# Fifteen short transfers ahead of the tenth K tile of a decode kernel

## The chip, the cores and the metric

The kernel runs on one core of one Trainium2 chip. The metric is the device time of one execution in microseconds; of three runs before the change the median is 377.65 (377.62 to 378.11). A profile is of one execution of its own; "span" is the time from its first to its last instruction.

## The reference

One decode step of a transformer block for 4 sequences, in bfloat16: attention over a window of the cache, then a gated MLP, each after a layer norm and each added to its input.

```python
W = min(4096, max(256, Sk // 4))                       # 4096 of 16384 cached positions
q = (layernorm(x) @ wq)                                # x: 4 x 576, 32 query heads of 128
k, v = k_cache[:, :, Sk - W:, :], v_cache[:, :, Sk - W:, :]   # 4 x 16 KV heads x 4096 x 128
p = softmax(q @ k.T * 128 ** -0.5)                     # two query heads share one KV head
h = x + (p @ v).reshape(4, 4096) @ wo
gate, up = layernorm(h) @ W_gate, layernorm(h) @ W_up  # 576 x 4608 each
h2 = h + (gate * (gate > 0) * up) @ W_down
```

The arithmetic is small; the data is not. K and V are 64 MB each, and with the weights the kernel reads about 160 MB from memory.

## The kernel before

The work has 16 groups of four KV heads (`NTILE`), four for each sequence. A group has one K tile and one V tile of 128 partitions by 16384 elements, 4 MB each. All tiles lie in one large SBUF tensor, `arena`, which has two parts: a head for the spread-out queries, and four slots of 4 MB (`NSLOT`, `TILE`) that are used in turn by `ring_slot`. Into the slots go first the weight wq, then K0 to K3, then K and V alternately (K4, V0, K5, V1 and so on: V trails K by four groups), then the last four V tiles. wo, W_gate, W_up and W_down are loaded after them into the space that has become free; W_down comes in five pieces.

Nearly all transfers are issued by one engine, SyncE (SP), in the order of the calls of `P.dma("sync", ...)`; x alone is loaded from ScalarE's queue. `place` keeps for each block of 64 columns who read it last, and makes the new transfer wait for that reader: K9, the tenth K tile, waits for the QK matmuls of K7, whose slot it takes. `Prog` records operations in a queue for each engine and writes them out by `emit`; a wait stands in front of the instruction and holds up everything behind it on that engine. Each transfer adds 16 to a semaphore when it is complete. SyncE's order around the change is K8, V4, K9, V5.

VectorE transposes each K tile in place (`turn_k`, L424), TensorE multiplies it with the queries (`pe_qk`, L448 and L34). After the four groups of a sequence follow the row maximum (L453), the exponential (L467), a rearrangement of the probabilities (`remap`, L475, L482, L487) and, group by group, the product with V (`pe_pv`, L509 and L34) and the picking of the wanted rows (`select_o`, L519 to L526). At the end stand the product with wo (L617), the norm, gate and up (L666), and the product with W_down (L690), whose pieces are waited for one by one. Then the output, 4 rows, is stored from SyncE (L710), which waits for its arrival.

Of the kernel before, what the change touches and what calls it, by code (L numbers as in the profile page):

```python
# [9 lines left out]
BF16 = mybir.dt.bfloat16  # L10
# [110 lines left out]
def bass_sequential_preLN__sliding_block_cached__glu_gated_reglu__decode_kernel(  # L121
# [12 lines left out]
    with ExitStack() as es:  # L134
        cnt = [0]

        def sb(name, shape, dt):
            return es.enter_context(nc.sbuf_tensor("sb_" + name, shape, dt))

        P = Prog()  # L140
# [5 lines left out]

        PPW = 6144
        AW = 2 * QWW + NSLOT * TILE
        arena = sb("arena", [128, AW], BF16)
        pp = sb("pp", [128, PPW], BF16)  # L150
        ident_b = sb("ident_b", [128, 128], BF16)
# [64 lines left out]
        def place(name, off, size, reader, make, key=None):  # L216
            deps = []
            for blk in range(off // 64, (off + size) // 64):
                r = owner.get(blk)
                if r is not None and r not in deps:  # L220
                    deps.append(r)
                owner[blk] = reader
            semk = key or "d_" + "_".join(str(v) for v in name)
            P.dma("sync", ("L",) + name, make, semk, deps)
            land[name] = off
# [3 lines left out]
        def ring_slot():  # L229
            s = ring[0] % NSLOT  # L230
            ring[0] += 1
            return s


        def add_kv(kind, g):
            b, qd = divmod(g, 4)
            s = ring_slot()
            off = slot0 + s * TILE
            cache = A_k_cache if kind == "K" else A_v_cache
            src = cache[b, 4 * qd:4 * qd + 4, SK - WIN:SK, :].rearrange("a (p t) d -> p a (t d)", p=32)  # L240
            place((kind, g), off, TILE, ("QK", g) if kind == "K" else ("PV", g),
                  lambda e: e.dma_start(out=arena[:, off:off + TILE], in_=src), key=f"slot{s}")  # L242


        def main_rows(W):
            return W[0:512, :].rearrange("(p r) n -> p (r n)", r=4)

        def last_rows(W):
# [5 lines left out]
        place(("wq", 0), wq_off, TILE, "QMM",  # L254
              lambda e: e.dma_start(out=arena[:, wq_off:wq_off + TILE], in_=main_rows(A_wq)), key=f"slot{s}")  # L255
        for g in range(NTILE):
            add_kv("K", g)
            if g >= 4:
                add_kv("V", g - 4)
# [3 lines left out]
        for g in range(NTILE - 4, NTILE):  # L263
# [5 lines left out]
        place(("gu", 0, 4), off, F, ("GU", 1, 4), lambda e, off=off: e.dma_start(  # L269
            out=bass.AP(tensor=arena, offset=off, ap=[[2 * AW, 64], [1, F]]), in_=B_W_gate[512:576, :]))  # L270
        P.dma("sync", ("L", "gu", 1, 4), lambda e, off=off: e.dma_start(
            out=bass.AP(tensor=arena, offset=AW + off, ap=[[2 * AW, 64], [1, F]]), in_=B_W_up[512:576, :]), "d_gu_1_4")
        gu_off[(0, 4)] = gu_off[(1, 4)] = off
# [8 lines left out]
        for r0, r1 in zip(WD_ROWS, WD_ROWS[1:]):  # L282
            place(("wd", r0), wd_off + r0 * D, (r1 - r0) * D, ("DOWN", 1),
                  lambda e, r0=r0, r1=r1: e.dma_start(
                      out=arena[:, wd_off + r0 * D:wd_off + r1 * D],
                      in_=B_W_down.rearrange("(p r) n -> p (r n)", p=128)[:, r0 * D:r1 * D]))
# [18 lines left out]
                                                in_=c_qm[:, :, :].rearrange("p q (h j) -> p q h j", j=4),  # L305
# [4 lines left out]
                                                in_=to_v[:, :, :].rearrange("p n (k a) -> p n k a", a=4),  # L310
# [14 lines left out]
        for sg in range(2):  # L325
            pool(f"c_toq{sg + 1}", lambda e, sg=sg: e.affine_select(
                out=toq[:, :, :, :], in_=toq[:, :, :, :],
# [84 lines left out]
        def put_q():  # L412
            for i in range(4):
                for q in range(2):
                    act("QW", lambda e, i=i, q=q: e.copy(  # L415
                        out=bass.AP(tensor=arena, offset=32 * i * AW + 2 * i + q, ap=[[AW, 32], [512, 16], [136, 4], [32, 4]]),
                        in_=bass.AP(tensor=q_keep, offset=q, ap=[[512, 32], [32, 16], [8, 4], [2, 4]])),
# [9 lines left out]
        def pe_qk(g):  # L427
            b, qd = divmod(g, 4)
            for cb in range(4):
                for w in range(2):  # L430
                    for a in range(4):
# [8 lines left out]
                        lhsT = arena[:, b * 2048 + cb * 512 + g % 4 * 128 + a * 32:][:, 0:32]  # L440
                        rhs = bass.AP(tensor=arena, offset=off, ap=[[AW, 128], [128, 64], [16, 4], [4, 2]])
                        out_ = bank[w][32 * a:32 * a + 32, :]
# [98 lines left out]
        def finish_o():  # L541
            for q in range(4):
                for qd in range(4):
# [17 lines left out]
                                              in_=bass.AP(tensor=e8, offset=0, ap=[[8, 128], [0, 4], [1, 8]])), ["c_e8", "c_selc0"])  # L561
# [47 lines left out]
        for a in range(8):  # L609
            for n in range(2):  # L610
                for j in range(4):
# [4 lines left out]
                    else:  # L616
# [6 lines left out]
                                             in_=bass.AP(tensor=psb, offset=512 + 224, ap=[[4096, 128], [1, 64], [0, 2]])), ["part1"])  # L623
# [54 lines left out]
        for i in range(2):  # L678
            dve(("HHT", i), lambda e, i=i: e.transpose(
                out=hhT[:, 576 * i:576 * i + 576].rearrange("p (r q) -> p r q", q=32),  # L680
                in_=bass.AP(tensor=pp, offset=3712 + 18 * i, ap=[[PPW, 128], [1, 18], [36, 32]])), [("HH", m) for m in range(3)])
# [26 lines left out]
        dve("OUT0", lambda e: e.tensor_copy(out=out_sb[:, 0:272], in_=bank[0][0:32, 0:272]), [("DOWN", 0)])  # L708
        act("OUT1", lambda e: e.copy(out=out_sb[:, 272:576], in_=bank[1][32:64, 0:304]), [("DOWN", 1)])  # L709
        P.dma("sync", "O", lambda e: e.dma_start(out=out.rearrange("b s d -> (b s) d"), in_=out_sb[0:B, :]), "d_out", ["OUT1", "OUT0"])  # L710
        P.op("sync", None, None, ["O"])
        P.emit(nc, es)


# [26 lines left out]
```

## Time and profile before

| | |
|---|---|
| median of 3 runs | 377.65 us |
| the profiled execution | 378.22 us |
| its span | 377.0 us |
| read from memory | 159.58 MB, 423 GB/s over the span |
| DMA packets | 6378, of them 728 under 512 bytes |
| granted TensorE clock, mean | 0.796 |
| VectorE busy | 228.8 us (61%) |
| TensorE busy | 213.8 us (57%) |

A transfer is cut into packets, which 16 DMA engines work off side by side, each in the order of its queue. A slice in the row of the DMA shares is a fortieth of the span; the digit 9 stands for 90% and more. K tiles land in the median 26.3 us after their issue and V tiles after 28.5, since each stands behind earlier ones in the queue. SyncE's rows in the timeline are its issues.

### The profile page before, as it was taken

Reading aid. Unit: us, or ns where it says so; the run is one execution under the profiler, and the core shown is the slowest. Engines: PE = TensorE matmul, PEld = TensorE weight load, DVE = VectorE, ACT = ScalarE, POOL = GpSimd, SP = SyncE. Lnnn points to the kernel's source line nnn. Section 1 sums busy time; section 2 is a strip of 40 time slices with the busy share of each in tenths; the row PEclk is TensorE's granted clock in tenths of the full one; section 3 lists DMA queues with packets and bytes.
Section 4 is the critical chain, followed back from the end, with each engine's and each line's share of the span. In section 5 each row is a group of like instructions: output and inputs, shape, how many; then the busy total and the mean of one; then the engine's idle time right before and its main releaser. Section 6 shows DMA issues by size and latency. Waiting matters only on the chain.

```text
span 377.0 us, 2556 instructions
## 1 busy us (share of the span) xinstructions
PE 213.8 (57%) x1462; PEld 39.9 (11%) x694; DVE 228.8 (61%) x164; ACT 53.7 (14%) x84; POOL 10.5 (3%) x29
## 2 busy tenths in 40 slices
PE   0404443239919091749282844664655787886658
PEld 0000000001001010001010100110000101002316
DVE  4088878779292969584847778665749433333240
ACT  3093000211000114010101140101010411112010
POOL 8200000000000000000000000000000000000000
PEclk9966666659969788696877786989695968998686
DMA  8999999999999999999999999999999999999996
GB/s 334 445 445 428 405 445 442 396 442 445 398 435 445 442 433 403 442 445 435 407 436 445 435 414 431 441 438 431 417 442 438 426 417 442 418 433 437 427 414 256
DMA packets 6378, 159.74 MB, mean 424 GB/s; under 512 B 728, under 2 KB 864, under 8 KB 1248
## 3 DMA queue, kind: packets, MB, share of 16 engines
q1 hardware_dynamic: 6360, 159.59, 98.7%
q8 instruction: 8, 0.13, 0.1%
q14 instruction: 2, 0.02, 0.0%
q10 hardware_dynamic: 8, 0.00, 0.0%
HBM read 159.58 MB, written 0.00 MB: 423 GB/s over the span
## 4 chain that ended last, share of the span: by engine, by line
DMA 60%; PE 20%; DVE 18%; SPq 1%; issue 0%; ACT 0%
DMA sb_arena<-in_A_k_cache_dram 53%; DVE sb_arena L424 16%; PE psb L34 11%; DMA sb_arena<-in_B_W_down_dram 7%; PE psb L448 4%; PE psb L509 3%; PE psb L690 2%; DVE sb_o_tmp L522 1%; DVE sb_pp L487 1%; SPq L242 0%; PE psb L475 0%; SPq L255 0%; ACT sb_out_sb L709 0%; SPq L251 0%; DVE sb_f L534 0%
## 5 line engine op out<-in xcount | busy, mean ns | idle before, releaser
L424 DVE STREAM_TRANSPOSE sb_arena<-sb_arena 128x8192 f32<-128x8192 f32 (+1 forms) x19 | 139.9, 7366 | 67.3 <-DMA sb_arena<-in_A_k_cache_dram 67.3
L448 PE MATMUL psb<-sb_arena 128*32 128x512 bf16 x256 | 42.8, 633 | 119.6 <-DVE sb_arena L424 119.5
L34 PE MATMUL psb<-sb_arena,sb_pp 128*128 128x512 bf16 (+1 forms) x386 | 108.7, 392 | 0.0
L509 PE MATMUL psb<-sb_arena,sb_pp 128*128 128x512 bf16 x128 | 50.8, 397 | 8.9 <-DVE sb_o_tmp L522 8.9
L519 ACT COPY sb_o_tmp<-psb 32x512 f32<-32x512 f32 x32 | 18.5, 577 | 182.0 <-PE psb L34 181.7
L34 PE MATMUL psb<-sb_arena 128*32 128x512 bf16 x256 | 43.6, 642 | 0.0
L522 DVE TENSOR_TENSOR sb_o_tmp<-psb,sb_fm 32x512 f32<-32x512 f32 x32 | 21.7, 678 | 18.6 <-PE psb L34 18.1
L448 PEld LDWEIGHTS psb<-sb_arena 128*32 128x32 bf16 x256 | 9.5, 119 | 161.9 <-DVE sb_arena L424 132.7
L509 PEld LDWEIGHTS psb<-sb_arena,sb_pp 128*128 128x128 bf16 x128 | 12.8, 100 | 116.6 <-issue 116.6
L526 DVE TENSOR_REDUCE sb_o_sel<-sb_o_tmp 128x128 f32<-128x512 f32 x16 | 17.7, 1106 | 0.5
L467 ACT ACTIVATE sb_pp<-psb,sb_hx 128x1024 bf16<-128x1024 f32 x4 | 4.5, 1113 | 79.4 <-DVE sb_hx L464 79.4
L487 DVE TENSOR_TENSOR sb_pp<-psb,sb_m 128x1024 bf16<-128x1024 f32 x8 | 9.3, 1206 | 4.9 <-PE psb L475 4.9
L482 ACT ACTIVATE sb_pp<-psb,sb_m 128x512 bf16<-128x512 f32 x16 | 9.7, 690 | 14.9 <-PE psb L475 14.9
L525 DVE TENSOR_TENSOR sb_o_tmp<-sb_o_tmp,sb_fm 64x512 f32<-64x512 f32 x16 | 11.0, 689 | 0.5
L415 ACT COPY sb_arena<-sb_q_keep 32x256 bf16<-32x256 bf16 x8 | 9.7, 1451 | 0.1
L690 PE MATMUL psb<-sb_arena,sb_pp 128*32 128x272 bf16 (+1 forms) x70 | 7.6, 396 | 3.7 <-DMA sb_arena<-in_B_W_down_dram 3.7
L401 DVE CAST sb_pp<-psb 128x512 bf16<-128x512 f32 x1 | 2.4, 2427 | 10.5 <-PE psb L381 10.5
L470 DVE STREAM_TRANSPOSE sb_pp<-sb_pp 128x1024 bf16<-128x1024 bf16 x4 | 5.0, 1245 | 5.1 <-ACT sb_pp L467 5.1
L475 PE MATMUL psb<-sb_pp,sb_to_v 128*32 128x256 bf16 x64 | 4.3, 400 | 6.3 <-DVE sb_pp L470 6.3
L690 PEld LDWEIGHTS psb<-sb_arena,sb_pp 128*32 128x32 bf16 x70 | 6.0, 131 | 5.1 <-DMA sb_arena<-in_B_W_down_dram 3.9
L34 PE MATMUL psb<-sb_arena,sb_hnT 128*32 128x384 bf16 x80 | 6.5, 407 | 0.0
L381 PE MATMUL psb<-sb_arena,sb_xnT 128*32 128x512 bf16 x16 | 2.6, 628 | 6.3 <-DMA sb_arena<-in_A_wq_dram 6.3
(120 smaller groups left out, 81.5 us busy)
## 6 DMA issues: line engine op xcount, KB each, us to landing
sb_arena<-in_A_k_cache_dram SPq DMA_DIRECT2D x16, 4096.0 KB, 26.3
sb_arena<-in_A_v_cache_dram SPq DMA_DIRECT2D x16, 4096.0 KB, 28.5
sb_arena<-in_A_wo_dram SPq DMA_DIRECT2D x1, 4608.0 KB, 24.8
sb_arena<-in_B_W_gate_dram SPq DMA_DIRECT2D x1, 4608.0 KB, 27.7
sb_arena<-in_A_wq_dram SPq DMA_DIRECT2D x1, 4096.0 KB, 12.7
sb_arena<-in_B_W_up_dram SPq DMA_DIRECT2D x1, 3456.0 KB, 27.3
sb_arena<-in_B_W_down_dram SPq DMA_DIRECT2D x1, 2160.0 KB, 26.5
sb_arena<-in_B_W_down_dram SPq DMA_DIRECT2D x1, 1440.0 KB, 29.6
```

Of the source, the lines that this page charges most:

```text
L34: return e.add_instruction(mybir.InstMatmult(name=e.bass.get_next_instruction_name(), engine=mybir.EngineType.PE, ins=[e.lower_ap(rhs), e. ...
L415: act("QW", lambda e, i=i, q=q: e.copy(out=bass.AP(tensor=arena, offset=32 * i * AW + 2 * i + q, ap=[[AW, 32], [512, 16], [136, 4], [32, 4]]),
L424: dve(("TRA", g), lambda e: e.transpose(out=dst, in_=src), [("L", "K", g)] if lo == 0 else [])
L448: fn = lambda e, out_=out_, lhsT=lhsT, rhs=rhs, start=start, stop=stop: e.matmul(out_, lhsT=lhsT, rhs=rhs, start=start, stop=stop, skip_gr ...
L482: act(("EV", b, 0), lambda e, a=a: e.activation(out=bass.AP(tensor=pp, offset=2 * a, ap=[[PPW, 128], [8, 2], [32, 128], [1, 2]]), in_=bank ...
L487: dve(("EV", b, 1), lambda e, n=n: e.tensor_tensor(out=bass.AP(tensor=pp, offset=16 + 8 * n, ap=[[PPW, 128], [32, 128], [2, 4], [1, 2]]), ...
L509: fn = lambda e, lhsT=lhsT, rhs=rhs, k=k, j=j: e.matmul(bank[2 + j], lhsT=lhsT, rhs=rhs, start=(k == 0), stop=(k == 7), skip_group_check=True)
L519: act(("OSC", g), lambda e, j=j: e.copy(out=o_tmp[32 * j:32 * j + 32, 0:512], in_=bank[2 + j][32 * j:32 * j + 32, :]), [("PV", g), ("OSEL" ...
L522: dve(("OSD", g), lambda e, j=j: e.tensor_tensor(out=ot(32 * j, 32), in0=bank[2 + j][32 * j:32 * j + 32, :].rearrange("p (t d) -> p t d", ...
L525: dve(("OS", g), lambda e: e.tensor_tensor(out=ot(64, 64), in0=ot(64, 64), in1=fmb(64, 64), op=ALU.mult), [("OSC", g)])
L526: dve(("OSEL", g), lambda e: e.tensor_reduce(out=o_sel[:, qd, b, :], in_=o_tmp[:, 0:512].rearrange("p (t d) -> p d t", d=DH), axis=AX.X, o ...
L690: return lambda e: e.matmul(out_, lhsT=lhsT, rhs=w[:, lo:hi], start=start, stop=stop, skip_group_check=True)
```

## The change

A scratch tile `mark` of 128 partitions by 1024 elements is allocated ahead of `arena`. After V4's issue and before K9's, SyncE issues fifteen transfers into it. The k-th, k from 1 to 15, copies k rows of wq, 40 + k elements (82 to 110 bytes) of each, to every fourth partition from the first on, at column 64 k. Together they have 120 rows. They wait for nothing and share one semaphore. Nobody reads `mark`; SyncE alone waits for the marks, after the output.

```diff
+        mark = sb("mark", [128, 1024], BF16)
         arena = sb("arena", [128, AW], BF16)
...
         for g in range(NTILE):
+            if g == 9:
+                for k in range(1, 16):
+                    P.dma("sync", ("L", "mark", k), lambda e, k=k: e.dma_start(
+                        out=bass.AP(tensor=mark, offset=64 * k, ap=[[4 * 1024, k], [1, 40 + k]]), in_=A_wq[0:k, 0:40 + k]), "d_mark")
             add_kv("K", g)
             if g >= 4:
                 add_kv("V", g - 4)
...
-        P.op("sync", None, None, ["O"])
+        P.op("sync", None, None, ["O", ("L", "mark", 15)])
```

## The prediction

> **What bounds the kernel now.** I read the page first: busy shares and the row of DMA shares, then the queues, then the chain that ended last.
>
> ```profile
> PE 213.8 (57%) x1462; PEld 39.9 (11%) x694; DVE 228.8 (61%) x164; ACT 53.7 (14%) x84; POOL 10.5 (3%) x29
> ...
> DMA  8999999999999999999999999999999999999996
> ...
> q1 hardware_dynamic: 6360, 159.59, 98.7%
> ...
> DMA 60%; PE 20%; DVE 18%; SPq 1%; issue 0%; ACT 0%
> ```
>
> No compute engine is busy for more than 61%, but the 16 DMA engines are busy in every slice, and the packets of SyncE's queue alone fill 98.7% of 16 engines' span. What a DMA engine has to do more is time; what an issuing or computing engine has to do more is not, so long as that queue stays full.
>
> Next, when SyncE issues, around the edit and at the end:
>
> ```profile
> 115.80 0.54 SPq L242 DMA_DIRECT2D sb_arena<-in_A_k_cache_dram  x1
> 122.80 0.54 SPq L242 DMA_DIRECT2D sb_arena<-in_A_v_cache_dram  x1
> 135.22 0.54 SPq L242 DMA_DIRECT2D sb_arena<-in_A_k_cache_dram  x1
> 142.22 0.54 SPq L242 DMA_DIRECT2D sb_arena<-in_A_v_cache_dram  x1
> ...
> 375.64 0.33 SPq L710 DMA_DIRECT2D out_dram<-sb_out_sb  x1
> ```
>
> The columns are start, duration, instruction. These are K8, V4, K9 and V5. Between V4's issue (ends 123.34) and K9's, SyncE stands 11.88 us waiting for the QK matmuls of K7 to free a slot.
>
> Third, the end of the kernel in the timeline:
>
> ```profile
> 367.49 7.24 PEld L690 LDWEIGHTS psb<-sb_arena,sb_pp 128*32 128x32 bf16 x70 [3.93 <-DMA sb_arena<-in_B_W_down_dram]
> ```
>
> The last product starts when the first piece of W_down lands. A DMA engine that is late to the end moves the end one for one.
>
> Last, the trace's packet records, one by one. A tile of 4 MB is 8 packets of 32768 bytes on each engine and then one of 4 bytes, the semaphore's. Sorting those 4-byte records by time and taking 16 per transfer gives each engine's lateness. K0's are 0.34 us apart from first to last. K9's lie from 159.32 to 161.00, apart by 1.68: ten engines within 0.14, then 0.19, 0.33, 1.01, 1.33, 1.63, 1.68. At the first piece of W_down the spread is 1.79, and seven engines lie between 1.66 and 1.79. The lag comes from the ten instruction-block packets after the start (eight of 16384 bytes, about 1 us each, at 46.3, 96.5, 140.0 us and on; two of 8192): a block makes one engine late, and a late engine never catches up. So the end belongs to the latest engine, and extra work on an early engine is free up to its lead.
>
> **The change part by part.** It moves and removes nothing; it adds four things.
>
> Fifteen issues on SyncE, after V4 and ahead of K9. They have no wait, so they run in the 11.88 us gap. Short transfers' nearest row is the output's 0.33 us for 4 rows, the dearest usual row is the K tile's 0.54: 15 x 0.33 = 5.0 to 15 x 0.54 = 8.1 us. Both fit. Behind them on SyncE stands K9, then V5 and the rest. Should the gap not do, there is a second cover: K9's packets start only when V4's are through, 149.64 to 151.28, so K9 may be issued some 14 us late before a ring runs dry. I take 0. Neither a gain nor a loss follows before that.
>
> 120 short packets (82 to 110 bytes each) and 120 semaphore packets on the DMA engines. How they spread is the first unknown. The only short transfer of the kernel with its own queue is the load of x, 4 rows of 1152 bytes:
>
> ```profile
> q10 hardware_dynamic: 8, 0.00, 7.4%
> ```
>
> That is four rows and four semaphores, and their records overlap (data at 2491, 2510, 2514 and 2567 ns): four rows, four engines. So the mark with k rows should use k engines. The Trainium skill, "DMA: Bandwidth & Descriptors", section on why a DMA increments its semaphore by 16, says so too, and adds that they are the lowest-numbered k; the four overlapping packets agree on the number, no run here shows which. By it the first engine carries 15 marks, the next 14, the sixteenth none. If they rotated, each engine would carry 7.5 on average.
>
> The price of one mark on an engine. In the last piece of W_down, packets of 1152 bytes start 47 ns apart, those of 4096 bytes of wq 155 ns apart, a semaphore takes 6 ns. The line through the two gives 4.7 ns plus 0.0367 ns a byte, so 8 ns for 96 bytes; with the semaphore 14 ns. That is the lower end: 15 x 14 = 0.21 us on the busiest engine. At the full 1152-byte pitch it is 15 x 53 = 0.80 us. The upper end comes from ordering: the semaphore reaches its waiter 0.36 us after its packet (wq's first: packet at 13.18, event at 13.54). If each mark had to be complete before the next began, one costs 0.36 + 0.05 = 0.41, and 15 cost 6.2 us. I take 14 ns: the nearest rows are short packets in a saturated stream, and between pieces of W_down the next data packet starts 6 ns after a semaphore, with no gap.
>
> What of it counts. A mark's delay shows at the end only as far as its engine is then among the latest. With 0.21 us falling to 0 over the engines and seven engines within 0.13 us of the last, the end moves 0 to 0.21; I take 0.15.
>
> One more wait on SyncE after the output has landed. The marks were done 220 us before, so it costs an instruction: adjacent issues stand 0.05 us apart (0.80 + 0.40 to 1.25). I take 0.05.
>
> The scratch tile moves every later tile by 2048 bytes per partition; their alignment below 2048 stays. No row shows an effect of position on a transfer (K and V packets take 1.21 us in all four slots). 0.
>
> Sum: +0.20 us. The profiled execution took 378.22 us (span 377.0 and 1.22 around it), 0.57 above the median; 378.4 there, **377.85** against the median of 377.65. A measurement of this kernel tells about 0.2% (0.75 us) from no change.
>
> **The rivals.**
>
> A, slower: marks don't pipeline. Each engine finishes one mark's write before its semaphore, and that before the next mark. For it: no two semaphores in this trace follow each other closer on one engine than the last W_down piece (8 x 47 + 6 ns = 0.38 us), so the stream of marks is something the trace never shows. Against it: no gap after any semaphore that it does show. The place is the ring between V4 and K9. With 0.1 us a mark the busiest engine is 1.5 us later, with 0.2 3.0, with 0.41 6.2, less the lead that it has over the last engine (0 to 1.7, half of it taken, 0.9). That gives 378.3, 379.8 and 383.0. It decides from about 0.11 us a mark: (0.75 + 0.9) / 15. The Trainium skill, "DMA: Bandwidth & Descriptors", section "Queues, rings and completion order", states that a semaphore write lands only after every earlier write of its engine, which is what such a stall would come from; the trace agrees that it lands late, 0.36 us, but shows following data unhindered. The Trainium skill's "DMA: Bandwidth & Descriptors", section "Anatomy of one DMA", puts a fixed 2.0 us on each DMA (of another issue path); 15 of them one after the other would by that be an estimated 30 us, and the last two pieces of W_down, 0.38 us apart on an engine, disagree.
>
> B, faster: the latest engine is relieved. Mean lag at W_down's first piece is about 0.9 of 1.79 us. If 240 added packets shift which engine fetches which instruction block, or when, so that the late ones are spared, up to 0.9 us is to be had: 376.8. For it: the ten blocks now fall on different engines and the latest are bunched. Against it: TensorE's program, which needs the blocks, is unchanged. It decides only if nearly all of the bunch goes.
>
> C, slower: SyncE is held. If a mark takes over 0.79 us to issue (11.88 / 15), K9 is issued late, and over 1.87 us each ((151.28 - 123.34) / 15) the rings run dry behind V4: 15 x 2.5 us would leave them empty for some 10 us, 388. Every single issue in the timeline lies between 0.33 and 0.68 us, so this has little.
>
> D, it doesn't do what it says: all rows of a mark on one engine. 120 x 8 + 15 x 6 ns = 1.05 us there, 378.4 with half the lead absorbed; the x load's four engines speak against it.
>
> **How the numbers follow.** Forecast, within 0.2%: 0.52 (D's 0.02 lies inside). A 0.36, C 0.02: slower 0.38. B 0.10: faster. The range is 377.0 to 381.0: below it B's greater part (0.08), above it A from 0.28 us a mark, and C (0.11 together).
>
> **What would show it.** On SyncE 15 new issues between 123.3 and about 131, K9 still at 135.2. In the packet records 120 packets of 82 to 110 bytes near 150 us. Spread of K9's semaphores 1.7 to 1.9 us (forecast); 3 and more, and lasting to the end, means A; DMA share below 9 near 150 us means C. A K9 tile that lands by 161.2 and a product that starts at 367.5 to 367.9 confirm the sum. What would make it wrong: a price of a mark that no row here has, or another drawing of instruction blocks.

## The result and the profile after

The changed kernel takes 379.82 us (median of 4 runs, 379.54 to 380.1), the kernel before 377.63 beside it: 1.0055 of it, 95% interval 1.0039 to 1.0071, or 2.2 us slower. It lies inside the stated range, but 2.0 us above the forecast of 377.85, where the range had been widened for rival A. The profiled execution took 379.72 us, with a span of 378.4.

The page of the changed kernel, the lines that answer to those of before (busy times, DMA shares, the queue, the chain that ended last):

```profile
PE 208.3 (55%) x1447; PEld 39.4 (10%) x694; DVE 228.3 (60%) x164; ACT 53.7 (14%) x84; POOL 10.5 (3%) x29
...
DMA  8999999999999999999999999999999999999995
...
q1 hardware_dynamic: 6600, 159.60, 98.4%
...
DMA 57%; PE 21%; DVE 20%; issue 1%; ACT 0%; SPq 0%
```

The queue has 240 packets more (120 rows, 120 semaphores), and no slice in the middle is below 9: at this grain nothing is to be seen. SyncE's issues in the timeline:

```profile
122.30 0.53 SPq L243 DMA_DIRECT2D sb_arena<-in_A_v_cache_dram  x1
122.87 11.27 SPq L260 DMA_DIRECT2D sb_mark<-in_A_wq_dram  x15
134.54 0.60 SPq L243 DMA_DIRECT2D sb_arena<-in_A_k_cache_dram  x1
```

The fifteen issues fill 11.27 us, nearly all of the gap of 11.7 us, and K9 is still issued on time. K9's transpose on VectorE, before and then after:

```profile
161.48 8.71 DVE L424 STREAM_TRANSPOSE sb_arena<-sb_arena 128x8192 f32<-128x8192 f32 x1 [5.08 <-DMA sb_arena<-in_A_k_cache_dram]
```

```profile
163.14 8.71 DVE L429 STREAM_TRANSPOSE sb_arena<-sb_arena 128x8192 f32<-128x8192 f32 x1 [7.34 <-DMA sb_arena<-in_A_k_cache_dram]
```

The wait in the bracket is 2.26 us longer (the whole execution ran 0.6 us ahead of before's until then). The product with W_down, the last consumer, before and then after:

```profile
367.49 4.74 PE L690 MATMUL psb<-sb_arena,sb_pp 128*32 128x272 bf16 x38 [3.72 <-DMA sb_arena<-in_B_W_down_dram]
```

```profile
369.02 5.08 PE L695 MATMUL psb<-sb_arena,sb_pp 128*32 128x272 bf16 x50 [3.71 <-DMA sb_arena<-in_B_W_down_dram]
```

It starts at 369.02 in place of 367.49, although the execution had been 0.6 us ahead until K9. So the loss comes at the marks and stays to the end.

The packet records say where. In the kernel before, K9's last semaphore comes 9.72 us after V4's last; with the change 12.01 (150.68 to 162.70): 2.29 us lost. Since mark k has rows of 80 + 2k bytes, the records tell the engines apart: k rows lie on k engines, and the engine that first appears with mark 1 has 15 of them. Each row and its semaphore pass in 14 to 15 ns where the engine was early. But the first K9 packets behind them take up to 2.46 us in place of 1.21. The table shows when each engine's first mark starts, and by how much the time from there to K9's semaphore is longer than 8 undisturbed packets of 1.21 us:

```
marks on the engine      15    14    13    12    11    10     9     8     7     6     5     4     3     2     1
first mark at, us      0.53  0.56  0.54  1.58  0.09  1.86  1.83  0.00  0.18  2.07  0.23  0.22  0.18  0.25  0.33
lost from there, us    1.74  1.91  2.19  2.20  1.53  1.96  2.20  1.11  0.50  1.18  0.51  0.49  0.44  0.41  0.29
```

The first row is counted from the first mark of the earliest engine, at 148.98 us. The loss grows with the marks. The sixteenth engine has no mark and lost 0.26 us all the same, here and when the change was run again, so a small part of the loss is not an engine's own; where that part comes from was not tried. Of the four engines that were late already, by 1.49 to 1.71 us at V4's semaphores, three have 9 to 12 marks; they start on them up to 0.4 us after their V4 and then lose about 2 us each. They set K9's landing and, since no engine catches up, the end.

### The profile page after: what moved, and what is told of

The parts are those of the page before. It is cut to its first block, busy times and chain, and to the rows that moved or that the text cites. A ratio compares the mean times of both kernels' runs of the same rounds, so it can differ in the third digit from the quotient of the medians.

```text
span 378.4 us, 2556 instructions
## 1 busy us (share of the span) xinstructions
PE 208.3 (55%) x1447; PEld 39.4 (10%) x694; DVE 228.3 (60%) x164; ACT 53.7 (14%) x84; POOL 10.5 (3%) x29
## 4 chain that ended last, share of the span: by engine, by line
DMA 57%; PE 21%; DVE 20%; issue 1%; ACT 0%; SPq 0%
DMA sb_arena<-in_A_k_cache_dram 48%; DVE sb_arena L429 16%; PE psb L34 13%; DMA sb_arena<-in_B_W_down_dram 9%; PE psb L453 4%; PE psb L514 3%; DVE sb_o_tmp L527 1%; DVE sb_pp L492 1%; PE psb L480 1%; PE psb L695 0%; DVE sb_pp L475 0%; DVE sb_hx L458 0%; ACT sb_pp L472 0%; SPq L289 0%; SPq L256 0%
## 5 line engine op out<-in xcount | busy, mean ns | idle before, releaser
L34 PE MATMUL psb<-sb_arena,sb_pp 128*128 128x512 bf16 x384 | 106.3, 385 | 2.9 <-issue 2.8
L514 PE MATMUL psb<-sb_arena,sb_pp 128*128 128x512 bf16 x115 | 44.0, 383 | 9.0 <-DVE sb_o_tmp L527 9.0
L695 PE MATMUL psb<-sb_arena,sb_pp 128*32 128x272 bf16 (+1 forms) x70 | 6.7, 352 | 4.5 <-DMA sb_arena<-in_B_W_down_dram 4.5
L680 DVE TENSOR_TENSOR sb_pp<-psb,sb_pp 128x384 bf16<-128x384 f32 x3 | 1.5, 550 | 9.0 <-PE psb L671 9.0
L671 PE MATMUL psb<-sb_arena,sb_hnT 128*32 128x384 bf16 x40 | 4.2, 405 | 4.0 <-DMA sb_arena<-in_B_W_up_dram 2.0
L34 PE MATMUL psb<-sb_arena,sb_hnT 128*32 128x384 bf16 x80 | 6.2, 392 | 0.0
```

Of the source, the lines that this page charges most:

```text
L34: return e.add_instruction(mybir.InstMatmult(name=e.bass.get_next_instruction_name(), engine=mybir.EngineType.PE, ins=[e.lower_ap(rhs), e. ...
L514: fn = lambda e, lhsT=lhsT, rhs=rhs, k=k, j=j: e.matmul(bank[2 + j], lhsT=lhsT, rhs=rhs, start=(k == 0), stop=(k == 7), skip_group_check=True)
```

## The experiments

Three theories were put to the test. S: each small transfer's completion (its semaphore, on the engine) takes its time, one after another. P: an engine looks ahead a limited number of packets, and short ones use them up. L: rows under 512 bytes are slow in themselves. Beside these: the moved tiles, the shared semaphore, contention among all engines. "Lost by the mean engine" is the mean of K9's 16 semaphores less that of K8's, less two undisturbed tiles (19.41 us); in the kernel before it is 0.01 us, with the change 1.27. Each ratio is to the kernel before on the same chip, with the 95% interval.

**The tile alone.**

```diff
-            if g == 9:
-                for k in range(1, 16):
-                    P.dma("sync", ("L", "mark", k), lambda e, k=k: e.dma_start(
...
-        P.op("sync", None, None, ["O", ("L", "mark", 15)])
+        P.op("sync", None, None, ["O"])
```

> The scratch tile is allocated, no transfer is issued; the output is the reference's. If the loss comes from the transfers, the time is that of before, 377.6 +- 0.4 us. If it comes from the 2048 bytes by which every later tile is moved, it is 379.8 as with the change.

1.0001 (0.9992 to 1.001). Moving the tiles by 2048 bytes costs nothing.

**One transfer of 256 short rows.**

```diff
-                for k in range(1, 16):
-                    P.dma("sync", ("L", "mark", k), lambda e, k=k: e.dma_start(
...
+                P.dma("sync", ("L", "mark", 15), lambda e: e.dma_start(
+                    out=bass.AP(tensor=mark, offset=0, ap=[[1024, 128], [64, 2], [1, 48]]),
+                    in_=A_wq[0:256, 0:48].rearrange("(p r) n -> p r n", r=2)), "d_mark")
```

> One transfer of 256 rows of 96 bytes in place of the fifteen: 16 short packets and 1 semaphore on each engine. In the changed kernel's packet records an engine with 1 to 5 marks lost 0.3 to 0.5 us, one with 9 to 15 lost 1.2 to 2.2 us. Theory S (the completion of each small transfer costs, so the loss goes with the semaphores): one completion, 0.3 us lost on each engine, 377.9. Theory P (an engine looks ahead a limited number of packets, and short ones use them up, whatever they are): 17 packets, like 8 or 9 marks, 1.1 to 2.2 us lost, 378.7 to 379.8. Theory L (rows under 512 bytes are slow in themselves): 16 of them, at least as much as 15 marks, 1.7 to 2.2 us, 379.4 to 379.8.

0.9999 (0.999 to 1.0009). The mean engine lost 0.20 us, of which 16 rows at 8 ns and a semaphore are 0.13. 16 short packets on each engine with one semaphore do not stall it: P and L, as put, fall.

**Eight transfers of 16 rows.**

```diff
-                for k in range(1, 16):
+                for k in range(8, 16):
                     P.dma("sync", ("L", "mark", k), lambda e, k=k: e.dma_start(
-                        out=bass.AP(tensor=mark, offset=64 * k, ap=[[4 * 1024, k], [1, 40 + k]]), in_=A_wq[0:k, 0:40 + k]), "d_mark")
+                        out=bass.AP(tensor=mark, offset=(k - 8) * 1024, ap=[[8 * 1024, 16], [1, 48]]),
+                        in_=A_wq[0:128, 0:48].rearrange("(r j) n -> j r n", j=8)[k - 8]), "d_mark")
```

> Eight transfers of 16 rows of 96 bytes in place of the fifteen: 8 short packets and 8 semaphores on each of the 16 engines. Theory S: as engines with 8 marks, 1.1 to 2.2 us lost on all, 378.7 to 379.8. Theory P: 16 packets, the same 1.1 to 2.2. Theory L: 8 short rows, half of the loss with 256 rows in one transfer. So this run against the one of 256 rows in one transfer tells S (this one far slower) from P (the same) and L (this one less).

1.0024 (1.0013 to 1.0035), 0.8 us. The mean engine lost 0.86 us, 0.75 over the packets. Half the rows of the run before it and eight times its semaphores: what costs is the transfer, not the row. That is S, but with less than it had said: 1.1 to 2.2 us were expected on every engine.

**Rows of 512 bytes.**

```diff
-        mark = sb("mark", [128, 1024], BF16)
+        mark = sb("mark", [128, 4096], BF16)
...
-                        out=bass.AP(tensor=mark, offset=64 * k, ap=[[4 * 1024, k], [1, 40 + k]]), in_=A_wq[0:k, 0:40 + k]), "d_mark")
+                        out=bass.AP(tensor=mark, offset=256 * k if k > 1 else 0, ap=[[4 * 4096, k], [1, 256 if k > 1 else 257]]),
+                        in_=A_wq[0:k, 0:256 if k > 1 else 257]), "d_mark")
```

> The fifteen transfers with rows of 512 bytes (514 in the one-row transfer) in place of 82 to 110. Same packets and semaphores. Theories S and P: the same loss as with the change, 1.7 to 2.2 us and 15 x 15 ns for the longer rows, 379.8 to 380.2. Theory L: the stall goes, 15 x 30 ns on the busiest engine, 377.6 to 378.1.

1.0033 (1.002 to 1.0046), 1.0 us; the mean engine lost 0.96. Less than the change's 1.27, and less than S had said; but the stall stays, where L let it go.

**A semaphore for each mark.**

```diff
-                        out=bass.AP(tensor=mark, offset=64 * k, ap=[[4 * 1024, k], [1, 40 + k]]), in_=A_wq[0:k, 0:40 + k]), "d_mark")
+                        out=bass.AP(tensor=mark, offset=64 * k, ap=[[4 * 1024, k], [1, 40 + k]]), in_=A_wq[0:k, 0:40 + k]), f"d_mark{k}")
...
-        P.op("sync", None, None, ["O", ("L", "mark", 15)])
+        P.op("sync", None, None, ["O"] + [("L", "mark", k) for k in range(1, 16)])
```

> The fifteen transfers as in the change, but each adds to a semaphore of its own. If what costs is that fifteen transfers in flight count on one semaphore, the loss goes: 0 to 0.2 us against before. If it is each transfer's completion whatever its semaphore (theory S), the loss stays: K9's last semaphore 2.0 to 2.5 us later than 9.7 us after V4's, as with the change, 1.7 to 2.3 us in all.

1.0047 (1.0035 to 1.006). The loss stays (mean engine 1.10 us): that they share a semaphore isn't it.

**The change again, on the same chip as the last.**

There is no edit against the changed kernel.

> The changed kernel once more, beside the others on the same chip: 1.7 to 2.3 us over before. Spread of K9's semaphores 2.5 to 3.5 us, loss of the mean engine 1.0 to 1.4 us. If the 2.2 us of the first measurement came from which engines were late in those runs, the loss of the latest engine differs while that of the mean engine stays.

1.0044 (1.0032 to 1.0057), mean engine 1.11 us, K9's spread 3.07. That is 1.6 us, just under the 1.7 to 2.3 expected; the loss is confirmed, and its interval overlaps with that of the first measurement.

**Fifteen, then thirty, transfers of one row.** All go to one engine.

```diff
-                        out=bass.AP(tensor=mark, offset=64 * k, ap=[[4 * 1024, k], [1, 40 + k]]), in_=A_wq[0:k, 0:40 + k]), "d_mark")
+                        out=bass.AP(tensor=mark, offset=64 * k, ap=[[1024, 1], [1, 47]]), in_=A_wq[0:1, 0:47]), "d_mark")
```

> Fifteen transfers of one row of 94 bytes: all on one engine, 15 short packets and 15 semaphores on it, none on the other 15. In the changed kernel the engine with 15 marks lost 1.7 us and was not late before. Theory S with the absorption that the prediction stated: this engine loses 1.5 to 2.2 us, but has a lead of 1.0 to 1.7 us over the latest, so K9's last semaphore and the end move by 0 to 1.2 us. If the loss is one of all engines together (contention, not a stall of the engine's own queue), the mean loss over 16 engines stays near 0.9 to 1.3 us and the end moves by 1.7 to 2.3; by S it is 1/16 of 2, about 0.1 us.

1.0015 (1.0006 to 1.0024), 0.56 us. The engine's 15 rows pass in 0.21 us, then its first two K9 packets take 2.55 and 1.79 us in place of 1.21: 2.13 us lost on it, 0.17 on the mean engine. The stall is one engine's own, and the lead that this engine had absorbed most of it: K9's last semaphore is 0.83 us late, the end 0.56.

Now thirty; SyncE's last wait is for the thirtieth.

```diff
-                for k in range(1, 16):
+                for k in range(30):
                     P.dma("sync", ("L", "mark", k), lambda e, k=k: e.dma_start(
-                        out=bass.AP(tensor=mark, offset=64 * k, ap=[[4 * 1024, k], [1, 40 + k]]), in_=A_wq[0:k, 0:40 + k]), "d_mark")
+                        out=bass.AP(tensor=mark, offset=(k % 15) * 64 + 1024 * (k // 15), ap=[[1024, 1], [1, 47]]), in_=A_wq[0:1, 0:47]), "d_mark")
```

> Thirty transfers of one row, all on one engine, where fifteen cost it 2.1 us and moved the end by 0.56. If the price is one of each transfer (0.13 us and 14 ns of packets): 4.2 us on this engine, its lead of some 1.4 us absorbed once, 2.3 to 3.0 us over before. If it is one stall of the queue that a longer row of transfers does not repeat: 2.4 us on this engine, 0.6 to 1.0 over before. Their issue takes some 15 us, 3 more than SyncE stands idle, so K9 is issued some 3 us late; its ring has 14 us of work left, and that is expected to cost nothing.

1.0086 (1.0073 to 1.01), 3.3 us, over the 2.3 to 3.0 of the theory of a price for each and far over the one stall of the other. The rows pass in 0.42 us, the first K9 packet then takes 5.10 us, the second 1.79: 4.89 us lost. K9's transpose and its wait:

```profile
164.67 8.71 DVE L429 STREAM_TRANSPOSE sb_arena<-sb_arena 128x8192 f32<-128x8192 f32 x1 [8.54 <-DMA sb_arena<-in_A_k_cache_dram]
```

The trace's semaphore events of these thirty transfers, all on one engine, give the price itself. At issue each posts an event at once (30 of them, from 124.37 on); the other 30 are the completions, in us:

```
150.336 150.521 150.705 150.890 151.075 151.259 151.444 151.629 151.814 151.999 ... 155.544 155.729
```

They come 184 or 185 ns apart (at most 192), though the packets that caused them passed 14 ns apart. Fifteen do the same in the run with fifteen. So the completions of one engine go one after another at 0.185 us each, and the tile behind is held for nearly as long: 30 x 0.185 = 5.55 us against 4.89 lost, 15 x 0.185 = 2.78 against 2.13. The difference, 0.66 and 0.65, does not grow with their number; we take it as what the engine absorbs once. For the engines that were early in the repeated change, 0.185 n - 0.66 gives with 15 marks 2.12 (measured 2.23), 14 1.93 (1.95), 13 1.75 (1.79), 11 1.38 (1.51), 8 0.82 (1.12), 7 0.64 (0.57), 5 0.27 (0.33); with 4 to 1 it gives next to nothing where 0.17 to 0.26 was lost, as much as on the engine without a mark. In the first profile of the change single engines lie up to 0.44 us beside it. Eight marks on every engine: 0.82 (0.86 for the mean). The Trainium skill, "DMA: Bandwidth & Descriptors", section "Queues, rings and completion order", says that a semaphore write lands only after every earlier write of its engine; the events, which come one after another and behind their packets, fit that, while the pace of 0.185 us is this trace's. The Trainium skill's section on why a DMA increments its semaphore by 16 (same page) says that the increments of the engines that a transfer does not use are posted at issue; the 30 early events agree.

**Rows between the completions.** Eight transfers of 128 rows, of 96 bytes and then of 512. The second edit shows only where it differs from the first.

```diff
-                for k in range(1, 16):
+                for k in range(8, 16):
                     P.dma("sync", ("L", "mark", k), lambda e, k=k: e.dma_start(
-                        out=bass.AP(tensor=mark, offset=64 * k, ap=[[4 * 1024, k], [1, 40 + k]]), in_=A_wq[0:k, 0:40 + k]), "d_mark")
+                        out=bass.AP(tensor=mark, offset=64 * k, ap=[[1024, 128], [1, 48]]), in_=A_wq[0:128, 0:48]), "d_mark")
```

> Eight transfers of 128 rows of 96 bytes: on each engine 8 times 8 short packets and a semaphore, so that semaphores stand some 72 ns apart instead of 14; 64 x 8 + 8 x 6 ns = 0.57 us of packets on each engine. The eight transfers of 16 rows lost 0.86 us on the mean engine, 0.11 of it packets. If each completion costs its time whatever is between them (0.75 us for eight): 1.3 us lost, 379.3 to 379.7 on this chip. If a completion takes some 0.1 us that the packets between two of them hide, the loss is little over the packets' time: 0.6 to 0.9 us.

1.0059 (1.0047 to 1.0072), 2.2 us. The mean engine lost 1.21 us, 0.57 of it packets, so 0.64 is left where sixteen-row transfers left 0.75: nearer to the theory that adds the two (1.3) than to the one that hides the completions (0.6 to 0.9). The time of 380.13 us is above what either expected.

These transfers were also slower to issue, so that K9 came late to the queue:

```profile
123.35 15.58 SPq L260 DMA_DIRECT2D sb_mark<-in_A_wq_dram  x8
138.97 0.55 SPq L243 DMA_DIRECT2D sb_arena<-in_A_k_cache_dram  x1
142.49 6.22 SPq L243 DMA_DIRECT2D sb_arena<-in_A_v_cache_dram  x1
```

The last two of the eight took 4.06 and 8.47 us. But K9 is still issued some 10 us before the first mark's packet at 149.32, so the loss does not come from there; it is the same with rows of 512 bytes (K9 issued at 138.51).

```diff
-        mark = sb("mark", [128, 1024], BF16)
+        mark = sb("mark", [128, 2048], BF16)
...
+                        out=bass.AP(tensor=mark, offset=256 * (k - 8), ap=[[2048, 128], [1, 256]]), in_=A_wq[0:128, 0:256]), "d_mark")
```

> Eight transfers of 128 rows of 512 bytes: semaphores stand 8 x 23.5 + 6 = 0.19 us apart on each engine, packets alone 1.55 us. Eight transfers of 16 rows of 96 bytes lost 0.75 us on the mean engine over their packets, eight of 128 rows of 96 bytes (0.07 us apart) 0.64. If a completion takes some 0.1 us that data between two of them hides: 1.5 to 1.7 us lost by the mean engine. If each small transfer costs 0.08 to 0.1 us over its packets whatever is between: 2.2 to 2.4 us. Time over before: the loss of the mean engine, or up to 1 us more where the latest engine loses most.

1.009 (1.0076 to 1.0104), 3.4 us; the mean engine lost 2.73 us, 1.18 over the packets' 1.55. More than either theory said. On an early engine a row of 512 bytes starts every 24 ns as reckoned, but over all engines a row's record lasts 33 ns on average and up to 342. How much of the 1.18 is completions and how much rows that wait is not told apart by this run. So it does not show that 0.19 us of data between two completions hides one.

**Other places.** Behind all data, that is not ahead of K9 but after the loop that issues the five pieces of W_down:

```diff
+        for k in range(1, 16):
+            P.dma("sync", ("L", "mark", k), lambda e, k=k: e.dma_start(
+                out=bass.AP(tensor=mark, offset=64 * k, ap=[[4 * 1024, k], [1, 40 + k]]), in_=A_wq[0:k, 0:40 + k]), "d_mark")
```

> The same fifteen transfers, issued behind the last piece of W_down instead of ahead of K9. Theory S (the stall lies in the order of SyncE's queue and makes late what stands behind): only the output stands behind, 1.3 us after the last piece has landed, so 0 to 0.3 us over before, and K9's spread as before, 1.7 to 2.0 us. If the transfers cost their time wherever they stand, 1.6 to 2.2 us over before.

0.9999 (0.999 to 1.0008). Where no tile stands behind the marks, their completions cost nothing. Their issue shows something else:

```profile
342.75 19.21 SPq L289 DMA_DIRECT2D sb_mark<-in_A_wq_dram  x15
```

It takes 19.21 us for what took 11.27, while eight tiles and pieces are outstanding; here nothing waits behind it. And from ScalarE's queue, again in place of those ahead of K9, in the loop over the groups:

```diff
             flush()
+            if g == 6:
+                for k in range(1, 16):
+                    P.dma("scalar", ("L", "mark", k), lambda e, k=k: e.dma_start(
+                        out=bass.AP(tensor=mark, offset=64 * k, ap=[[4 * 1024, k], [1, 40 + k]]), in_=A_wq[0:k, 0:40 + k]), "d_mark")
```

> The same fifteen transfers issued from ScalarE's queue, some 20 us earlier, in a stretch of 18 us in which ScalarE only waits. They come one each 0.7 us on a queue of their own, beside the K and V packets. If the stall lies in the order of SyncE's queue, the K and V packets go on meanwhile: 0.1 us of packets on the mean engine, K9's last semaphore and the end within 0.3 us of before. If each small transfer costs an engine its 0.13 us on whatever queue, 7.5 of them cost the mean engine 1.0 us, and the end moves by 1 to 2.

1.0001 (0.9993 to 1.001). The marks' packets pass from 107.05 to 137.53 us. From K6's semaphores to K8's, the stretch around them, the mean engine lost 0.15 us against before; 7.5 marks of 14 ns are 0.11 of it.

```profile
103.10 0.99 ACTq L597 DMA_DIRECT2D sb_mark<-in_A_wq_dram  x2
...
104.13 10.04 ACTq L597 DMA_DIRECT2D sb_mark<-in_A_wq_dram  x13
```

The same fifteen transfers, in the midst of the K and V stream, for nothing. This run changed the queue, the place in the stream, and with the queue the spacing. The packets of the two queues take turns on an engine: a K or V packet of 1.21 us stands between a mark's row and its semaphore. So the fifteen marks of the busiest engine start 1.23 to 2.44 us apart, though they are issued 0.73 us apart, and no completion has to wait 0.185 us for another. That fits the account above; whether the same spacing within SyncE's own queue would save as much was not tried.

## Why the prediction was right and wrong

Right: what bounds the kernel, and that only the time of the DMA engines counts. The end follows the last packet of the latest engine, an early engine's loss is absorbed by its lead (fifteen rows on one engine: 2.13 us lost, 0.56 at the end), and the loss lasts to the end. The spread of the marks, k rows on k engines, is what the sizes show. The tile and its 2048 bytes cost nothing. D falls with the sizes; C did not come about, with less to spare than stated: a mark takes 0.48 to 0.80 us to issue, median 0.72, not 0.33 to 0.54, so the sum is 11.27 us and not 5 to 8, in a gap of 11.7. C's own first threshold was 0.79 us a mark. The second cover, the work left in the rings, held with thirty marks: K9's issue then ended only at 139.78, and the loss is still that of the completions.

Wrong: the price of one mark on its engine, which the sum takes as 14 ns. The step read this from packet records of a stream whose semaphores stand 0.38 us apart or more, and took "no gap after a semaphore" to mean "completions are free". The 14 ns is right for the packets; the completion behind it takes 185 ns, and a row of fifteen cannot hide that. So +0.15 us became +2.2, and the time came out inside the range only because the range reached over to A. Rival A had the cause, completions one after another, and, at 0.2 us a mark, 379.8, though not the place: a mark's packets do not wait for the mark before (14 ns apart), the tile behind them does. As for A's prices, its upper end of 0.41, from the 0.36 us between packet and event, was a delay and not a rate: 0.36 says when an event comes, 0.185 how soon the next can.

Wrong too in A: "half of the lead absorbs 0.9". The end moved by 2.2 because three of the late engines carried 9 to 12 marks and lost some 2 us from the first of them on. That is 0.18 to 0.24 us for each mark (0.16 to 0.20 when the change was run again, where they lost 1.8 to 1.9), without the full 0.66 that early engines absorb; their marks also come 0.3 to 0.7 us apart at first. Why late engines fare so stays open. A's 379.8 at 0.2 us meets the measured 379.82 so closely by luck: more was lost on late engines than the 0.9 taken off allows, and fewer marks stood on them than fifteen. B didn't show: the latest were not relieved.

Three small slips of the prediction change nothing. D's 1.05 us less half the lead (0.9) gives about 377.8, not 378.4. The mean lag at W_down's first piece, B's ground, is 1.0 us by the packet records and not 0.9. And of the four rows of x the last starts 2 ns after the third has ended; that four engines carry them is shown by the four semaphores.

## What to carry to other kernels

In a kernel that keeps its DMA queue full, count the transfers that come in a row, and not only their bytes: in this kernel each cost every engine that it used some 0.19 us of completion, hidden behind a large tile but not behind other small transfers. Put many small rows into one transfer (256 rows cost 0.2 us an engine), put small transfers behind the last tile, or issue them from another engine's queue, where here K and V packets went between them. When a trace is to give a price, look for a row in which the thing stands as close to its like as the change would put it.

## What was not expected of the hardware

The completions of one engine come 0.185 us apart to within 8 ns, while the packets pass in 14 ns. And issues can take long where much is outstanding: with thirty marks queued, the last three of these took 1.2 to 2.4 us each, and SyncE's K9 and V5 2.36 and 4.92 us in place of 0.54:

```profile
123.76 13.61 SPq L260 DMA_DIRECT2D sb_mark<-in_A_wq_dram  x30
137.42 2.36 SPq L243 DMA_DIRECT2D sb_arena<-in_A_k_cache_dram  x1
142.15 4.92 SPq L243 DMA_DIRECT2D sb_arena<-in_A_v_cache_dram  x1
```

What it is that holds them back was not tried.

The issue of a mark has its price too, and not by its bytes. In the change a mark of 4 rows takes 0.63 us to issue and one of 15 rows 0.80, more than a K tile of 4 MB at 0.54. Transfers of one row take 0.25 us (the first of a series 0.49), those of 16 rows 0.59 and, while nothing holds them back, those of 128 rows 0.43.
